# Four small moves in a hand-written instruction order: batch 7's attention beside the crossed products

## The chip, the cores and the metric

The kernel runs on one core of a Trainium2 chip. A core has five engines that run their own instruction lists in order and meet only at semaphores: TensorE (matrix products, shown as PE, its weight loads as PEld), VectorE (DVE), ScalarE (ACT), GpSimd (POOL) and SyncE (SP, which here only issues transfers). The metric is the device time of one execution in microseconds (us).

## The reference

Two layers follow one another. The first is a linear attention over 8 batches, 8 heads, 576 positions and 64 channels; the second mixes positions through a rank of 32 and then channels through two matrices, with a residual.

```python
r = relu(x);  phi(x) = concat([r * cos_w, r * sin_w])      # 64 -> 128 features
q_p, k_p = phi(q), phi(k)
kv  = einsum('bhsf,bhsd->bhfd', k_p, v)
num = einsum('bhsf,bhfd->bhsd', q_p, kv)
den = einsum('bhsf,bhf->bhs', q_p, k_p.sum(2)) + 1e-6
x   = (num / den), heads side by side                       # [8, 576, 512]

u   = x + ((x^T @ U) @ V)^T                                 # rank 32 over positions
out = u + relu(u @ w_ch1) @ w_ch2                           # 512 -> 2048 -> 512
```

## The kernel before

**Tiles.** A batch has 576 positions: four chunks of 128 (c = 0 to 3) and a tail of 64 (c = 4). The tails of two batches make one tile of 128, so there are four pairs of tails. The first matrix has 16 column blocks of 128 (j), each a `g1_main` unit: four products of 128x512 (L579) and a relu on ScalarE (L588). The second matrix is worked through in two halves per batch by `half_part`: seven products per half, where a plain product would need eight, each a group of eight matmuls of 128x256 (L891). Their operand sums (`hid_sum`, L833) are on VectorE. For batch 7, and for blocks 4 to 7 and 12 to 15 of batch 6, the first matrix is worked through with seven products (`g1_cross`, L676), with sums of uT and of the weights (L611, `uT_sum`, `w1_sum`).

**The crossed steps.** In `g1_cross` and `g1_join`, a block p has a bank "xy" (columns 0 to 255 are X, the rest is Y) and a bank Z. `opened` writes products 1 (X) and 2 (Y), then ScalarE casts X to `kept` ("P1") and VectorE adds it to Y ("C11"). `sixth` accumulates product 6 on X and casts it ("U2"); `fifth` writes Z and casts it ("P5"); `third` accumulates on X, and VectorE adds it to P5 ("C22"); `closed` accumulates on Z and X, followed by the add "C12" and a relu on VectorE, and a relu on ScalarE.

**Attention of a later batch.** `attention_plan` spreads the next batch's attention over the slots of the batches before it. For batch 7 (base slot 189) it holds two kv units, five x units (chunk order 4, 0, 1, 2, 3), the A unit (x^T U, L445), u (`u_mm`, L475, and `u_add`, L483), the tails' u (`u_tail`, L497 and L504) and transposes on SP's queue (`utr_dma`, L521 and L527). An x unit is eight matmuls (L422) into a tile of two banks tagged "X", then on VectorE rec, a reciprocal and the normalisation (L412, L413, L432). `u_mm` for columns 0 to 2, `u_mm` for column 3, and `u_tail` likewise, take this same X tile, so each waits for what reads it.

**The order.** It is written out by hand. `slots` is a list of TensorE steps; `todo[i]` holds what is issued right behind slot i. The instructions of a slot go to the engines in program order, so a slot number says both when a step's matmuls come and where its VectorE, ScalarE and SP work stands in those engines' queues. Batch 6's first stage begins at slot 188: two g1 units, then in turn a `half_part` of batch 5 (even slots) and a unit of batch 6 (odd slots). Slots 218 to 220 are `tail_late(2)`, the last `closed` of batch 6 and `tail_late(3)`: units of the first matrix for the tails of batches 4 and 5. From slot 221 on the groups of batch 7's crossed products alternate with `half_part` of batch 6. The number of slots up to here also sets where `uT_sum` of batch 7 and the operand sums of batch 6 are placed (`at`).

Of the kernel before, what the change touches and what calls it, by code (L numbers as in the profile page):

```python
# [17 lines left out]
def kernel(  # L18
# [13 lines left out]
    B = 8  # L32
# [13 lines left out]
    def tail(b):  # L46
        lo = TS * (b % 2)
        return slice(lo, lo + TS)
# [290 lines left out]
    def kv_unit(b, hg, tag, bufs, eng=None, n=E):  # L339
        if b not in kv_sb:  # L340
            kv_sb[b] = pool.tile([P, H, E], BF16, tag="kv", bufs=2, name="kv")
        acc = ps.tile([P, 4, n], FP32, tag=tag, bufs=bufs, name="kv_ps")
        vx = v_ext
        for i in range(4):
            h = hg * 4 + i
            for c in range(5):
                nc.tensor.matmul(  # L347
                    out=acc[:, i, :],
                    lhsT=k_of(b, c, h),
                    rhs=v_tl[:, h, 0:n] if c == 4 and b < 2  # L350
                    else vx[:, c if c < 4 else 4 + b % 2, h, 0:n],
                    start=(c == 0),
                    stop=(c == 4),
                )
        cast(eng or V_, kv_sb[b][:, hg * 4 : hg * 4 + 4, 0:n], acc)
# [83 lines left out]
    def A_of(b):  # L439
        return A_sb[b % 4]  # L440
# [16 lines left out]
    def four_banks(*spare):  # L457
        t = ps.tile([P, 2, 512], FP32, tag="X", bufs=1, name="va4_ps")
        more = [
            x if not isinstance(x, tuple)  # L460
            else ps.tile([P, 512], FP32, tag=x[0], bufs=x[1], name="va_ps")
            for x in spare
        ]
        return [t[:, 0, :], t[:, 1, :]] + more
# [3 lines left out]
    def u_mm(b, *spare, js=range(4)):  # L468
        if b not in u_bf:
            u_bf[b] = pool.tile([P, 4, 4, P], BF16, tag="u_bf", bufs=3, name="u_bf")  # L470
        va.setdefault(b, {}).update(zip(js, four_banks(*spare)))
        for c in range(4):
            for j in js:
                rows = slice(j * R, j * R + R)
                nc.tensor.matmul(  # L475
                    out=va[b][j][:, c * P : c * P + P], lhsT=V_bf[rows, c, :],
                    rhs=A_of(b)[rows, :], start=(c == 0), stop=(c == 3),
                    tile_position=(j * R, 0),
                )
# [8 lines left out]
    def u_tail(pr, *spare, js=range(4)):  # L488
        if pr not in u_tl:
            u_tl[pr] = pool.tile(  # L490
                [P, DM], BF16, tag="k_p" if pr == 3 else "u_tl", bufs=1, name="u_tl"
            )
        vt = dict(zip(js, four_banks(*spare)))
        for i in range(2):
            for j in js:
                rows = slice(j * R, j * R + R)
                nc.tensor.matmul(  # L497
                    out=vt[j][tail(i), 0:P], lhsT=V_tl[rows, :],
                    rhs=A_of(2 * pr + i)[rows, :], start=True, stop=True,
                    tile_position=(j * R, i * TS),  # L500
                )
        for j in js:
            ns = slice(j * P, j * P + P)
            nc.vector.tensor_tensor(  # L504
                out=u_tl[pr][:, ns], in0=x_tl[:, ns], in1=vt[j][:, 0:P], op=ALU.add
            )
# [475 lines left out]
    def spare(at):  # L982
        if at < 72:
            return ("o", 2) if 32 <= at < 52 else ("g", 3)
        return ("o", 2) if at < 88 else ("s", 1)
# [14 lines left out]
    def attention_plan(b):  # L1000

        plan = []
        if b < 4:
            w, f_at, q_eng, k_eng, qtr, lo = PLAN[b]
        else:
            w, q_at, k_at, qtr, lo = PLAN[b]

        def put(at, f, *a, tag=False):
            if tag:
                a = a + spare(w + at)  # L1010
            plan.append((w + at, lambda: f(b, *a)))

        for n, c in enumerate(QORD):
            if b > 3:
                put(q_at[0] + q_at[1] * n, q_prep, c, q_at[2:])
                put(k_at[0] + k_at[1] * n, k_prep, c, k_at[2:])
                put(k_at[0] + (3 * n) // 2, v_prep, 0, H, (c,), (G_,))
                continue
            if b == 3:
                q_eng, k_eng = V_ if n == 3 else A_, A_ if n < 3 else None  # L1020
                put((-12, -11, -10, -7, -3)[n], q_prep, c, (q_eng, q_eng))
                put(n - 9 if n < 3 else -5, k_prep, c, (A_, k_eng))
                if n > 2:
                    put(2 * n - 12, k_prep, c, (None, V_))
                put(-4 if n > 2 else -6, v_prep, 0, H, (c,), (A_ if n > 2 else G_,))
                continue
            put(f_at + ((n - 1) % 5 if b == 2 else n), q_prep, c, (q_eng, q_eng))
            put(f_at + 6 + n, k_prep, c, (k_eng, k_eng))
            put((-6, -2, -1, -5, -5)[n], v_prep, 0, H, (c,), (V_ if n > 2 else A_,))
        for n, (c0, c1) in enumerate(((4, 5), (0, 2), (2, 4))):  # L1030
            at = qtr[n] if b > 4 else 1 if b == 3 and n == 2 else qtr + 2 * n
            put(at, qtr_dma, c0, c1)
        plan.append((w + (b == 2), lambda: kv_unit(b, 0, *spare(w), A_ if b > 2 else V_)))
        plan.append((w + 2, lambda: kv_unit(b, 1, *spare(w + 2), A_ if b > 2 else V_)))
        for n, c in enumerate(ORD):
            if b > 3:
                put(4 + 2 * n, x_unit, c, "X", 1)
            elif n % 2:
                put(9 if (b, n) == (3, 3) else 4 + (3 * n) // 2, x_two, c, tag=True)
            else:  # L1040
                put(4 + (3 * n) // 2, x_unit, c, "X", 1)
        a_at = 15 - b if b < 4 else 14
        if b == B - 1:
            put(a_at, A_unit, "s", 1, A_)
        else:
            put(a_at, A_unit, tag=True)
        odd = b % 2 == 1


        def two(at):  # L1050
            return [T1, ("s", 1)] if at >= 88 else [spare(at)] * 2

        if b == B - 1:
            plan.append((w + a_at + 2, lambda: u_mm(b, ("s", 1), js=(0, 1, 2))))
            plan.append((w + a_at + 4, lambda: u_mm(b, js=(3,))))
        else:
            plan.append((w + a_at + 2, lambda: u_mm(b, *two(w + a_at + 2))))
        for j in range(4):
            put(a_at + 2 + j + (2 if b > 4 and j > 1 else 0), u_add, j)
        put(a_at + 3, utr_dma, 0, 2)  # L1060
        put(a_at + (7 if b > 4 else 5), utr_dma, 2, 4)
        if odd:
            if b == B - 1:
                plan.append((w + a_at + 9, lambda: u_tail(b // 2, ("s", 1), js=(0, 1, 2))))
                plan.append((w + a_at + 10, lambda: u_tail(b // 2, js=(3,))))
            else:
                plan.append((w + a_at + 9, lambda: u_tail(b // 2, *two(w + a_at + 9))))
            put(a_at + 10, utr_dma, 4, 5)
        for at, t in zip(lo, loads(b + 1) if lo else ()):
            plan.append((w + at, t))  # L1070
        return plan
# [264 lines left out]
    slots, todo = [], {}  # L1336

    def put(at, thunk):
        todo.setdefault(at, []).append(thunk)

    def sums(b, n, ats):
        for i, at in enumerate(ats):
            put(at, lambda i=i: hid_sum(b, n, i + 1))
# [31 lines left out]
    for b in range(3, B - 2):  # L1375
        at = len(slots)
# [15 lines left out]
    b6, b7 = B - 2, B - 1  # L1392
# [30 lines left out]
    def crossed(*steps):  # L1423
        def go():
            for f, b, p in steps:
                f(b, p)

        return go
# [9 lines left out]

    at = len(slots)
    sums(b6 - 1, 0, (at, at + 1, at + 3))  # L1440
    sums(b6 - 1, 1, (at + 13, at + 15, at + 19))
    for i, half, sl in (
        (1, 1, -8), (2, 1, -6), (3, 1, -4), (1, 0, -3), (4, 1, -2), (3, 0, -1), (2, 0, 11), (4, 0, 23),
    ):
# [15 lines left out]
    def tail_late(j):  # L1460
        if j == 2:
            t = ps.tile([P, 2, 512], FP32, tag="X", bufs=1, name="gt_ps")[:, 0, :]
        else:
            t = ps.tile([P, 512], FP32, tag="s", bufs=1, name="gt_ps")
        g1_tail(2, j, t.rearrange("p (j t) -> p j t", j=4))

    slots.append(lambda: tail_late(2))
    slots.append(crossed((closed, b6, 7)))
    slots.append(lambda: tail_late(3))

    at = len(slots)
    for i in range(4):
# [16 lines left out]

    for i, go in enumerate(groups):  # L1490
        slots.append(go)
        if i < 14:
            beside_g(b6, i)
        else:
            slots.append(lambda j=i - 14: tail_cross(j))
    at = len(slots)
# [16 lines left out]
    at = len(slots)  # L1513
# [19 lines left out]
    for b in range(2, B):  # L1533
        for at, t in attention_plan(b):
            put(at, t)
# [37 lines left out]
```

## Time and profile before

| what | value |
|---|---|
| median of 3 runs | 296.16 us (296.05 to 298.54) |
| the profiled execution's own time | 296.26 us |
| its span, first to last instruction | 294.5 us |
| mean granted TensorE clock | 0.997 |
| busy: PE, PEld | 284.8 us, 194.6 us |
| busy: DVE, ACT, POOL | 207.5 us, 169.3 us, 57.8 us |
| slots 192 to 203 in the trace | about 213.4 to 226.8 us |
| batch 7's first crossed step | 242.74 us |
| start of the last stage (`half_part` of batch 7 alone) | 271.85 us |
| last TensorE group starts, last VectorE add | 289.31 us, 290.39 us |

Rows of the trace name an engine, a source line, an operation and its tiles (`a_ps` is the A unit's accumulator, `va_ps` that of u and the tails' u, `c_ps` of the crossed products, `h_ps` of `half_part`, `S` an operand sum). Where many steps share a helper, they have that helper's line, and tiles and order tell them apart. The bracket at the end of a row is the time that the engine stood idle ahead of it, and what ended that. A busy TensorE may still wait inside: matmuls are pipelined, and the end of one overlaps the start of the next.

### The profile page before, as it was taken

The page shows a single profiled execution, that of the slowest core. Times are in us where ns is not written, and L with a number is a line of the kernel's source. Part 1 is how long each engine was busy: PE and PEld are TensorE (multiplying, and loading weights), DVE is VectorE, ACT ScalarE, POOL GpSimd, SP SyncE. Part 2 cuts the span into 40 slices and gives each one's busy share as a digit, 9 for nine tenths or more (in the row PEclk, how much of TensorE's full clock was granted, in tenths as well). Part 3 has the DMA queues.
Part 4 walks back from the last instruction along what each step waited for, and adds up shares of the span by engine and source line. Part 5 has one row for each costly group of instructions (what it writes and reads, how often), then busy time and mean ns, then how long its engine had stood idle before and what let it go on. Part 6 is the DMA issues. An engine that isn't in the chain of part 4 may idle for free.

```text
span 294.5 us, 7310 instructions
## 1 busy us (share of the span) xinstructions
PE 284.8 (97%) x2910; PEld 194.6 (66%) x2944; DVE 207.5 (70%) x503; ACT 169.3 (57%) x353; POOL 57.8 (20%) x92
## 2 busy tenths in 40 slices
PE   8999999999999999999999999999998999999994
PEld 3775554447545446766766666766776778889883
DVE  5977855596875698566457774779866877775773
ACT  3955742276782767488647764687643546557210
POOL 6520600000020005103200500042103213303330
PEclk9999999999999999999999999999999999999998
DMA  7999999899998989997899759874902744336023
GB/s 232 297 254 251 273 166 212 217 298 232 351 190 200 288 183 262 265 304 237 145 246 270 201 119 270 214 257 92 213 1 39 145 89 108 48 98 137 9 101 116
DMA packets 95174, 56.18 MB, mean 191 GB/s; under 512 B 58692, under 2 KB 91844, under 8 KB 95140
## 3 DMA queue, kind: packets, MB, share of 16 engines
q1 hardware_dynamic: 84420, 43.94, 59.7%
q0 software_dynamic: 10528, 11.57, 19.6%
q8 instruction: 23, 0.38, 0.5%
q10 hardware_dynamic: 192, 0.20, 0.2%
q14 instruction: 11, 0.09, 0.1%
HBM read 36.86 MB, written 9.44 MB: 157 GB/s over the span
## 4 chain that ended last, share of the span: by engine, by line
PE 94%; DVE 3%; issue 1%; ACT 0%; DVEq 0%
PE g_ps L579 29%; PE h_ps L891 26%; PE o_ps L759 10%; PE c_ps L676 6%; PE gt_ps L719 5%; PE kv_ps L347 3%; PE w_ps L234 3%; PE x_ps L422 3%; PE h_ps L759 1%; PE a_ps L445 1%; PE g_ps L596 1%; PE va_ps L475 1%; PE t_ps L365 1%; PE t_ps L377 1%; PE z_ps L1236 1%
## 5 line engine op out<-in xcount | busy, mean ns | idle before, releaser
L579 PE MATMUL g_ps<-uT,w_bf 128*128 128x512 bf16 x378 | 95.5, 380 | 1.1
L588 ACT ACTIVATE hid<-g_ps 128x512 bf16<-128x512 f32 x104 | 61.0, 598 | 57.1 <-PE g_ps L579 56.3
L579 PEld LDWEIGHTS <-w_bf 128*128 128x128 bf16 x402 | 37.8, 98 | 34.7 <-issue 0.2
L891 PEld LDWEIGHTS <-hid 128*128 128x128 bf16 x480 | 45.3, 98 | 9.0
L891 PE MATMUL h_ps<-w_bf,hid 128*128 128x256 bf16 x288 | 37.1, 273 | 0.0
L759 PE MATMUL o_ps<-w_bf,hid 128*128 128x512 bf16 x122 | 29.5, 380 | 0.4 <-issue 0.2
L131 POOL CAST v_ext<-vst 128x512 bf16<-128x512 f32 (+1 forms) x23 | 15.5, 700 | 58.2 <-issue 25.7
L891 PE MATMUL h_ps<-w_s,S 128*128 128x256 bf16 x208 | 26.5, 273 | 0.0
L891 PE MATMUL h_ps<-w_s,hid 128*128 128x256 bf16 x192 | 24.9, 273 | 0.0
L611 DVE TENSOR_TENSOR hid<-kept,c_ps 128x256 bf16<-128x256 f32 x36 | 14.2, 418 | 12.5 <-ACT kept L129 9.1
L847 DVE TENSOR_TENSOR o_sb<-o_sb,h_ps 128x256 f32<-128x256 f32 (+1 forms) x36 | 15.4, 431 | 10.7 <-PE h_ps L891 8.3
L891 PEld LDWEIGHTS <-S 128*128 128x128 bf16 x208 | 19.9, 98 | 4.0
L950 POOL DMA_DIRECT2D out_dram<-o_sb x16 | 10.1, 631 | 62.8 <-DVE o_sb L847 51.7
L483 DVE TENSOR_TENSOR u_bf<-x_bf,va_ps 128x512 bf16<-128x512 bf16 x27 | 17.6, 680 | 6.5 <-PE va_ps L475 2.8
L847 DVE TENSOR_TENSOR o_sb<-u_bf,h_ps 128x256 f32<-128x256 bf16 x28 | 11.7, 416 | 13.2 <-PE h_ps L891 13.2
L759 PEld LDWEIGHTS <-hid 128*128 128x128 bf16 x128 | 11.5, 98 | 12.2
L949 POOL DMA_DIRECT2D o_sb<-u_bf x8 | 10.4, 1295 | 36.6 <-DVE o_sb L847 35.5
L719 PE MATMUL gt_ps<-uT_tl,w_bf 128*128 128x128 bf16 x256 | 16.2, 219 | 0.0
L432 DVE TENSOR_TENSOR x_bf<-x_ps,rec 128x512 bf16<-128x512 f32 x22 | 15.2, 691 | 0.8
L719 PEld LDWEIGHTS <-w_bf 128*128 128x128 bf16 x256 | 15.1, 98 | 0.7
L129 ACT ACTIVATE kept<-c_ps 128x256 f32<-128x256 f32 x36 | 12.5, 380 | 4.9 <-PE c_ps L676 4.1
L306 ACT ACTIVATE k_p<-kst,cosw 128x512 bf16<-128x512 f32 x20 | 14.2, 713 | 0.1
(189 smaller groups left out, 457.6 us busy)
## 6 DMA issues: line engine op xcount, KB each, us to landing
qst<-in_q_dram SPq DMA_DIRECT2D x14, 512.0 KB, 5.4
kst<-in_k_dram SPq DMA_DIRECT2D x14, 512.0 KB, 6.5
vst<-in_v_dram SPq DMA_DIRECT2D x12, 512.0 KB, 6.7
out_dram<-o_sb POOLq DMA_DIRECT2D x19, 256.0 KB, 4.1
out_dram<-o_sb SPq DMA_DIRECT2D x16, 256.0 KB, 2.6
w_bf<-in_moe_w_ch_dram POOLq DMA_DIRECT2D x7, 512.0 KB, 12.4
o_sb<-u_bf POOLq DMA_DIRECT2D x8, 256.0 KB, 3.6
qst<-in_q_dram SPq DMA_DIRECT2D x2, 640.0 KB, 13.6
```

The costliest lines, as they stand in the source:

```text
L131: eng.tensor_copy(out=o, in_=i)
L306: nc.scalar.activation(out=o, in_=i, func=AF.Relu, bias=0.0, scale=w)
L432: nc.vector.tensor_tensor(out=x_of(b, c, rows).rearrange("p (g i d) -> p g i d", g=2, d=D), in0=view[:, :, :, 0:D], in1=rec[rows].unsqueez ...
L483: nc.vector.tensor_tensor(out=u_bf[b][:, j, :, :], in0=x_bf[b][:, :, ns], in1=va[b][j].rearrange("p (c n) -> p c n", c=4), op=ALU.add,)
L579: nc.tensor.matmul(out=g_ps.rearrange("p (c t) -> p c t", c=4), lhsT=w1_bf[:, d, j * P : j * P + P], rhs=uT[b][:, d, :, :], start=(d == 0) ...
L588: nc.scalar.activation(out=hid[b][:, j, :], in_=g_ps, func=AF.Relu, bias=0.0, scale=1.0)
L611: V_.tensor_tensor(out=o, in0=x, in1=y, op=op)
L676: nc.tensor.matmul(out=w[to].rearrange("p (c t) -> p c t", c=2), lhsT=lhs[:, d, cs], rhs=rhs[:, d], start=(first and d == 0), stop=(d == 1 ...
L719: nc.tensor.matmul(out=g_ps[:, jj, :], lhsT=w1_bf[:, d, j * P : j * P + P], rhs=uT_tl[pr][:, d, :], start=(d == 0), stop=(d == 3),)
L759: nc.tensor.matmul(out=o[:, cols], lhsT=lhs[:, j, c * P : c * P + P], rhs=w2_bf[:, j, cols], start=(j == 0), stop=(j == NJ - 1),)
L847: eng.tensor_tensor(out=o, in0=x, in1=y, op=ALU.add)
L891: nc.tensor.matmul(out=acc, lhsT=lhs[:, j, :], rhs=rhs[:, j, :], start=(j == 0 and at is not None), stop=(j == 7), skip_group_check=at is ...
```

## The change

Five parts of the order change; no arithmetic does.

- Batch 7's five x units go from slots 193, 195, 197, 199, 201 to 192, 194, 196, 198, 200.
- The first two operand sums of the second half of batch 5 go from slots 201 and 203 to 202 and 204.
- Column 3 of batch 7's `u_mm` goes from slot 207 to 208, behind the `half_part` of slot 208. Its `u_add` stays at slot 210.
- Column 3 of the last pair's `u_tail` goes from slot 213 to 214, and the transpose of that pair's tails with it.
- `tail_late(3)` goes from slot 220 to 221, behind the first group of batch 7 (`opened(7, 0)`), which goes from 221 to 220. Because `at` is taken ahead of it, batch 7's four uT sums go from slots 217 to 220 to 216 to 219, and the sums of batch 6 from 221, 222, 227 and 234, 236, 240 to 220, 221, 226 and 233, 235, 239. From slot 222 on the TensorE steps have their old numbers.

```diff
-                put(4 + 2 * n, x_unit, c, "X", 1)
+                put((3 if b == B - 1 else 4) + 2 * n, x_unit, c, "X", 1)
...
-            plan.append((w + a_at + 4, lambda: u_mm(b, js=(3,))))
+            plan.append((w + a_at + 5, lambda: u_mm(b, js=(3,))))
...
-                plan.append((w + a_at + 10, lambda: u_tail(b // 2, js=(3,))))
+                plan.append((w + a_at + 11, lambda: u_tail(b // 2, js=(3,))))
...
-            put(a_at + 10, utr_dma, 4, 5)
+            put(a_at + (11 if b == B - 1 else 10), utr_dma, 4, 5)
...
-    sums(b6 - 1, 1, (at + 13, at + 15, at + 19))
+    sums(b6 - 1, 1, (at + 14, at + 16, at + 19))
...
     slots.append(lambda: tail_late(2))
     slots.append(crossed((closed, b6, 7)))
-    slots.append(lambda: tail_late(3))
 
     at = len(slots)
...
     for i, go in enumerate(groups):
         slots.append(go)
+        if i == 0:
+            slots.append(lambda: tail_late(3))
         if i < 14:
             beside_g(b6, i)
```

## The prediction, made before the result was known

> **What bounds the kernel now.** I read the page's busy times and chain first, then TensorE's waits, then the order of time of TensorE, VectorE and ScalarE between 213 and 245 us, where all the edits lie.
>
> ```profile
> PE 284.8 (97%) x2910; PEld 194.6 (66%) x2944; DVE 207.5 (70%) x503; ACT 169.3 (57%) x353; POOL 57.8 (20%) x92
> PE 94%; DVE 3%; issue 1%; ACT 0%; DVEq 0%
> ```
>
> TensorE carries 94% of the chain that ended last, so the matmuls stay and only its stalls can go. Three of the six waits in its list lie here:
>
> ```profile
> PE a_ps L445 <- DVE x_bf L432: 0.9, 1, 0.9
> PE va_ps L497 <- DVE u_tl L504: 0.5, 1, 0.5
> PE va_ps L475 <- DVE u_bf L483: 0.5, 1, 0.5
> ```
>
> In TensorE's order of time the columns are start, duration and operation. Groups overlap, so I work with steps from one start to the next: 0.87 us for a g1 unit (x4, 128x512) or a product of half_part (x8, 128x256), 0.26 for an x unit, 0.22 for one crossed product (x2).
>
> ```profile
> 222.30 1.03 PE L579 MATMUL g_ps<-uT,w_bf 128*128 128x512 bf16 x4
> 223.17 0.60 PE L676 MATMUL c_ps<-uT,w_bf 128*128 128x256 bf16 x4
> 223.60 0.42 PE L422 MATMUL x_ps<-kv,q_pT 128*128 128x65 bf16 x8
> 223.86 1.04 PE L891 MATMUL h_ps<-w_s,hid 128*128 128x256 bf16 x8
> 225.02 0.38 PE L676 MATMUL c_ps<-uT_s,w_s 128*128 128x256 bf16 x2
> ...
> 226.66 0.24 PE L445 MATMUL a_ps<-x_bf,U_bf 128*32 128x128 bf16 x4 [0.93 <-DVE x_bf L432]
> ...
> 231.18 0.39 PE L475 MATMUL va_ps<-A_sb,V_bf 32*128 32x128 bf16 x4 [0.46 <-DVE u_bf L483]
> ...
> 237.49 0.24 PE L497 MATMUL va_ps<-A_sb,V_tl 32*64 32x128 bf16 x2 [0.50 <-DVE u_tl L504]
> ```
>
> There is a fourth stall that the list of waits does not name: 243.17 + 0.87 = 244.04, but the next group starts at 244.31. VectorE's order of time shows what each one waited for:
>
> ```profile
> 224.55 0.42 DVE L611 TENSOR_TENSOR hid<-kept,c_ps 128x256 bf16<-128x256 f32 x1 [1.46 <-ACT kept L129]
> 224.88 0.69 DVE L833 TENSOR_TENSOR S<-hid 128x1024 bf16<-128x1024 bf16 x1
> ...
> 225.92 0.69 DVE L432 TENSOR_TENSOR x_bf<-x_ps,rec 128x512 bf16<-128x512 f32 x1
> ...
> 230.44 0.68 DVE L483 TENSOR_TENSOR u_bf<-x_bf,va_ps 128x512 bf16<-128x512 bf16 x1
> ...
> 243.84 0.42 DVE L611 TENSOR_TENSOR hid<-kept,c_ps 128x256 bf16<-128x256 f32 x1 [0.33 <-ACT kept L129]
> ```
>
> The last x normalisation (225.92 to 226.61) stood behind the first join (224.55) and an operand sum (224.88), though its matmuls were over at 224.02. The group at 244.31 began 0.05 us after the join of 243.84 ended.
>
> **The change part by part.** No instruction is added or removed; the gain can only come from these stalls.
>
> *x units a slot sooner.* Each x unit now runs ahead of its slot's g1 unit. The first starts at 213.39 + 0.87 = 214.26; its kv cast on ScalarE ended at 213.98. VectorE follows: output add at 214.52, operand sum 214.86, then rec, reciprocal and x_tl from 215.19 at the old steps (0.21, 0.23, 0.69), ending at 216.32. x(0) needs that bank; the old start came 0.15 after the release (217.04, 217.19), so it starts at 216.47 where TensorE is ready at 216.26. That is a wait of 0.21, against 0.07 before. The later x units have 0.3 or more to spare. Slot 201's crossed products then end at 224.01 in place of 223.86: -0.15.
>
> Now a wait grows. The sixth product (225.02) starts 0.05 after the join of 224.55 ended. The chain to it starts with the g1 unit's relu and runs on through the P1 cast and that join. The x unit used to fill 0.26 of this time and is gone from there. New chain: g1 at 222.71, relu 1.07 later at 223.78 to 224.38, P1 cast 0.16 later (as before, 223.97 to 224.13) until 224.92, join 224.96 to 225.38, sixth product at 225.43. TensorE is free at 224.88, so it waits 0.55, against 0.29 before.
>
> Behind it, batch 7's A unit no longer waits: x(3) is normalised by about 224.1, ahead of the join in VectorE's order. Sixth product 0.22, change of operation 0.09, A unit 0.39 (as at 193.93 to 194.32): half_part starts at 226.13 in place of 226.84. **Gain 0.71.** The 0.16 ahead of the cast may belong to the x unit that moved; without it the gain is 0.87. The first join reads columns 256 to 511 of the bank and the sixth product writes columns 0 to 255. If only columns counted, the P1 cast (ended 224.51, +0.05) would release it, and the gain would be 1.17. I take 0.71, since 225.02 follows the join by the 0.05 us of the other releases.
>
> The Trainium skill, PSUM — Partial Sum Buffer, section Terms, speaks against this part in the same way: TensorE writing and VectorE reading one bank and quadrant at once is an error, so the scheduler must hold the product behind the join whatever the columns. By that rule the part gives 0.71, without it 1.17; the row at 225.02 agrees with the rule.
>
> *The two sums.* They moved from slots 201 and 203 to 202 and 204. Only ScalarE casts lie between on the evacuating engines, so VectorE's order is unchanged, and with the x work gone it reaches them sooner, with 1.56 us of idle behind them: nothing. A reordering cost could not exceed that idle.
>
> *u's last part a slot later.* Before, TensorE is ready at 230.56 and would start at 230.66 (0.10 for a change of operation, as 228.59 to 228.69), but it waits until 231.18 for the add of 230.44, which frees the X banks. After, half_part fills this time: 230.56 + 0.87 + 0.10 + 0.32 = 231.85 for the next crossed product, before 232.39. **Gain 0.54**; the cover left is 231.53 against 231.12, 0.41 us. The join after it has less cover: VectorE is free at 232.92, the join would start at 232.96. The last add stays at slot 210, so the transpose issued behind it on SP's queue keeps its place.
>
> *The tails' u a slot later.* Before: ready 236.82, start 237.49, half_part 237.66, next crossed product 238.53. After: 236.82 + 0.87 + 0.10 + 0.17 = 237.96, 0.57 sooner. Then the closing product (0.22 later, 238.18) meets the C22 join that ended at 238.30; with 0.05 that costs 0.17. **Gain 0.40** (0.57 if that join comes sooner). On SP only the tails' transpose moves, and its readers start at 266.71.
>
> *Batch 7's first step ahead of the last late tail unit.* The tail unit (0.90) now fills the time to the join. P1 cast, join (0.42) and 0.05 end well within the 0.90 + 0.87 us to the next product: **gain 0.27**. Cover 0.36 us, by VectorE: this step and the uT sums are a slot sooner, so a sum goes ahead of the C12 join. Batch 6's sums are one slot sooner too; only the third passes a join, into VectorE's idle 0.57 us at 247.57. ScalarE's evacuation of the tail unit (0.60) now follows the cast, and its bank is next wanted two groups later.
>
> Sum 0.71 + 0.54 + 0.40 + 0.27 = 1.92. From 244.31 on the order is the same and TensorE leads, so all of it should reach the end. The profiled execution took 296.26 (span 294.5 and 1.76 around it): 296.26 - 1.92 = 294.34, **294.3 us**. The median shown is 296.16, 0.10 less.
>
> **The rivals.** *VectorE takes over as the bound.* It is busy 6.00 of the 6.81 us from 232.39 to 239.20, nearly all one stretch behind the join of 233.50. If the join there comes no sooner, the second and third gains are lost: 0.98 is left, 295.3. Against: VectorE stood idle 0.52 ahead of that join, and 1.56 ahead of 228.77.
>
> *Slower: the transpose of batch 7's second half.* The first step needs both halves of uT, and now runs 2.56 us sooner (242.74 to 240.18), while the transpose, issued at 235.5, is 1.25 sooner. VectorE's second sum would start at 239.65, 5.4 us after the issue at 234.25. The trace shows landings of 2.7 and 4.2 us for uT, and 8.5 in the median for the larger q_pT. At 8.5 it lands at 242.75; two sums, the C12 join and its relu (0.42, 0.45, 0.45 and 0.50 in steps) bring half_part to about 244.6 in place of 241.51: 3.1 lost, 297.4. It starts to cost beyond 5.4 us and eats the whole gain at about 7.3. Unlikely, since nothing else of this size moves on SP.
>
> *No change that counts:* the saved waits return one group later because accumulator banks, not the named joins, are short: 296.2. The first stall alone speaks against it, as its bank chain was followed above.
>
> *More:* the gains of 1.17 and 0.57 come true: 293.7.
>
> **How the numbers follow.** Forecast 0.60; VectorE 0.20; no change 0.09; more 0.06; slower 0.05. From 293.6, just under the best sum, to 296.1, short of no change, holds some 0.85. A difference of 1% (2.96 us) is about what a measurement tells from none. Faster by that needs 293.2, beyond the best sum by 0.5: 0.05. Slower comes from the transpose, in which 297.4 is itself only 0.4% up, so it keeps 0.03.
>
> **What would show it.** Right: no wait of a_ps, and none of va_ps on u_bf or u_tl; the sixth product at about 225.4, the next half_part near 226.1; the product of 244.31 near 242.4; equal spacing from there. A longer gap ahead of the sixth product, or joins that begin with VectorE busy, would show the first rival; uT sums or opened products that wait for a DMA near 240 the second. Wrong altogether would be a start of the last stage (271.85) that does not move by about 1.9.

## The result, and the profile after

| | before | after |
|---|---|---|
| median | 296.62 us (10 runs) | 294.63 us (10 runs) |
| ratio, 95% interval | | 0.9933 (0.991 to 0.9957) |
| profiled execution, its span | 296.26, 294.5 us | 294.76, 293.0 us |
| start of slot 192's half_part | 213.39 us | 213.67 us |
| start of the last stage | 271.85 us | 270.33 us |
| between these two ("the stretch") | 58.46 us | 56.66 us |

The kernel is 1.99 us faster by the medians. All edits lie in the stretch, and there it gained 1.80; what comes ahead of the stretch was 0.28 longer in this execution, although no instruction there changed. The rows of the kernel before from which the stretch and its steps are read:

```profile
213.39 1.04 PE L891 MATMUL h_ps<-w_bf,hid 128*128 128x256 bf16 x8
...
226.84 1.05 PE L891 MATMUL h_ps<-w_bf,hid 128*128 128x256 bf16 x8
...
232.39 0.60 PE L676 MATMUL c_ps<-uT,w_bf 128*128 128x256 bf16 x4
...
239.20 1.04 PE L891 MATMUL h_ps<-w_s,hid 128*128 128x256 bf16 x8
...
243.17 1.04 PE L891 MATMUL h_ps<-w_bf,hid 128*128 128x256 bf16 x8
244.31 0.60 PE L676 MATMUL c_ps<-uT_s,w_s 128*128 128x256 bf16 x4
...
271.85 1.91 PE L891 MATMUL h_ps<-w_bf,hid 128*128 128x256 bf16 x16
```

The page of the changed kernel, busy times:

```profile
PE 284.9 (97%) x2910; PEld 194.5 (66%) x2944; DVE 206.6 (71%) x503; ACT 169.2 (58%) x353; POOL 56.6 (19%) x92
```

TensorE did the same work in a shorter span. Its list of waits in the changed kernel (engine, operation, releaser: total, times, longest):

```profile
PE c_ps L676 <- DVE hid L611: 0.4, 1, 0.4
PE x_ps L422 <- DVE x_tl L432: 0.2, 1, 0.2
```

The waits of a_ps on x_bf and of va_ps on u_bf and u_tl are gone, and two others have come. The order of time of TensorE in the changed kernel (start, duration, operation, idle time ahead); 0.28 has to be taken off a start to set it against one of before:

```profile
213.67 1.04 PE L891 MATMUL h_ps<-w_bf,hid 128*128 128x256 bf16 x8
...
215.67 1.04 PE L891 MATMUL h_ps<-w_s,S 128*128 128x256 bf16 x8
216.87 0.42 PE L422 MATMUL x_ps<-kv,q_pT 128*128 128x65 bf16 x8 [0.17 <-DVE x_tl L432]
...
223.97 0.60 PE L676 MATMUL c_ps<-uT,w_bf 128*128 128x256 bf16 x4
224.41 1.04 PE L891 MATMUL h_ps<-w_s,hid 128*128 128x256 bf16 x8
225.82 0.38 PE L676 MATMUL c_ps<-uT_s,w_s 128*128 128x256 bf16 x2 [0.38 <-DVE hid L611]
...
226.53 1.05 PE L891 MATMUL h_ps<-w_bf,hid 128*128 128x256 bf16 x8
...
231.22 0.39 PE L475 MATMUL va_ps<-A_sb,V_bf 32*128 32x128 bf16 x4
231.54 0.61 PE L676 MATMUL c_ps<-uT,w_bf 128*128 128x256 bf16 x4
...
237.13 0.39 PE L676 MATMUL c_ps<-uT,w_s 128*128 128x256 bf16 x2
237.52 0.38 PE L676 MATMUL c_ps<-uT_s,w_bf 128*128 128x256 bf16 x2
...
237.95 1.04 PE L891 MATMUL h_ps<-w_s,hid 128*128 128x256 bf16 x8
...
241.92 1.04 PE L891 MATMUL h_ps<-w_bf,hid 128*128 128x256 bf16 x8
242.79 0.60 PE L676 MATMUL c_ps<-uT_s,w_s 128*128 128x256 bf16 x4
...
270.33 1.91 PE L891 MATMUL h_ps<-w_bf,hid 128*128 128x256 bf16 x16
```

Reading it with the steps of the prediction: x(0), the second x unit, at 216.87 is 0.33 later than its half_part lets it (215.67 + 0.87); the sixth product at 225.82 is 0.54 later than 224.41 + 0.87; u's last part now starts straight behind its half_part; the closing product comes 0.39 behind the one ahead, in place of 0.22; and 242.79 follows 241.92 by the plain 0.87, so the fourth stall is gone.

VectorE's order of time in the changed kernel:

```profile
215.14 0.42 DVE L611 TENSOR_TENSOR uT_s<-uT,uT_s 128x512 bf16<-128x512 bf16 x1
215.59 0.17 DVE L412 TENSOR_SCALAR rec<-x_ps 64x8 f32<-64x8 f32 x1
...
216.03 0.69 DVE L432 TENSOR_TENSOR x_tl<-x_ps,rec 64x512 bf16<-64x512 f32 x1
...
223.85 0.69 DVE L432 TENSOR_TENSOR x_bf<-x_ps,rec 128x512 bf16<-128x512 f32 x1
225.35 0.42 DVE L611 TENSOR_TENSOR hid<-kept,c_ps 128x256 bf16<-128x256 f32 x1 [0.80 <-ACT kept L129]
```

The last x normalisation (223.85) now stands ahead of the join (225.35), so the A unit finds it done. The join ends at 225.77 and the sixth product starts at 225.82.

### The profile page after: what moved, and what is told of

It reads as the page before. It is cut to its first block, busy times and chain, and to the rows that moved or that the text cites. A ratio compares the mean times of both kernels' runs of the same rounds, so it can differ in the third digit from the quotient of the medians.

```text
span 293.0 us, 7309 instructions
## 1 busy us (share of the span) xinstructions
PE 284.9 (97%) x2910; PEld 194.5 (66%) x2944; DVE 206.6 (71%) x503; ACT 169.2 (58%) x353; POOL 56.6 (19%) x92
## 4 chain that ended last, share of the span: by engine, by line
PE 91%; ACT 3%; DMA 2%; DVE 2%; issue 1%; ACTq 0%; DVEq 0%
PE g_ps L579 29%; PE h_ps L891 26%; PE o_ps L759 10%; PE c_ps L676 7%; PE gt_ps L719 5%; PE kv_ps L347 3%; PE x_ps L422 3%; DMA qst<-in_q_dram 2%; PE a_ps L445 1%; PE h_ps L759 1%; PE g_ps L596 1%; PE va_ps L475 1%; PE t_ps L365 1%; ACT q_p L306 1%; ACT k_p L306 1%
## 5 line engine op out<-in xcount | busy, mean ns | idle before, releaser
L891 PEld LDWEIGHTS <-hid 128*128 128x128 bf16 x480 | 45.6, 98 | 9.5
L891 PE MATMUL h_ps<-w_bf,hid 128*128 128x256 bf16 x288 | 37.1, 273 | 0.0
L891 PE MATMUL h_ps<-w_s,S 128*128 128x256 bf16 x208 | 26.5, 272 | 0.0
L891 PE MATMUL h_ps<-w_s,hid 128*128 128x256 bf16 x192 | 24.9, 273 | 0.0
L891 PEld LDWEIGHTS <-S 128*128 128x128 bf16 x208 | 20.1, 98 | 4.4
```

What stands on the lines that cost most here:

```text
L891: nc.tensor.matmul(out=acc, lhsT=lhs[:, j, :], rhs=rhs[:, j, :], start=(j == 0 and at is not None), stop=(j == 7), skip_group_check=at is ...
```

## The experiments

The runs are compared by the stretch, from slot 192's half_part to the first product of the last stage. It came out as 56.66 in both profiles of the changed kernel, while whole times of one kernel spread over 2 us.

### Each part alone

The four parts that could gain were put into the kernel before one at a time.

```diff
 x alone
-                put(4 + 2 * n, x_unit, c, "X", 1)
+                put((3 if b == B - 1 else 4) + 2 * n, x_unit, c, "X", 1)
 u alone
-            plan.append((w + a_at + 4, lambda: u_mm(b, js=(3,))))
+            plan.append((w + a_at + 5, lambda: u_mm(b, js=(3,))))
 tails' u alone
-                plan.append((w + a_at + 10, lambda: u_tail(b // 2, js=(3,))))
+                plan.append((w + a_at + 11, lambda: u_tail(b // 2, js=(3,))))
...
-            put(a_at + 10, utr_dma, 4, 5)
+            put(a_at + (11 if b == B - 1 else 10), utr_dma, 4, 5)
 first step alone
-    slots.append(lambda: tail_late(3))
...
+        if i == 0:
+            slots.append(lambda: tail_late(3))
```

> Only the x units of batch 7 a slot sooner; the rest as before. Measured by one stretch of the profile: from the start of slot 192's product of half_part to the first product of the last stage (58.46 us before, 56.66 after the whole change). Theory A (separate TensorE stalls that add up): the a_ps wait of 0.93 goes, the sixth product's wait grows from 0.29 to about 0.55, x(0) waits 0.2 to 0.3; the stretch is 0.59 shorter, 57.87. Rival (columns, not the bank, hold the sixth product): 1.0 or more shorter. Rival (VectorE is the bound behind it): the va_ps waits on u_bf and u_tl grow by what is saved, the stretch stays within 0.15 of 58.46.

> Only column 3 of batch 7's u a slot later. Same stretch (58.46 us before). Theory A: the va_ps wait on u_bf goes and nothing comes in its place, 0.54 shorter, 57.92. Rival (VectorE is the bound): the join that began at 233.50 comes no sooner, so the waits on u_tl or of the closing products grow; the gain is under 0.2.

> Only column 3 of the tails' u and its transpose a slot later. Same stretch (58.46 us before). Theory A: the va_ps wait on u_tl goes (0.57), the closing product of slot 215 waits about 0.17 for the C22 join in its place: 0.40 shorter, 58.06. Rival (the join comes soon enough): 0.57 shorter, 57.89. Rival (VectorE bound): under 0.15.

> Only batch 7's first step ahead of the last late tail unit, with the sums that move with it. Same stretch (58.46 us before). Theory A: the gap of 0.27 ahead of the next crossed product goes, 58.19. Rival (the transpose of batch 7's second half is needed too soon): uT sums or the opened products wait for a DMA, the stretch is no shorter or grows by up to 3.

| part | forecast | alone: stretch, gain | inside the whole change |
|---|---|---|---|
| x units | 0.71 | 57.85, 0.61 | 0.59 |
| u's last part | 0.54 | 57.92, 0.54 | 0.54 |
| tails' u | 0.40 | 58.03, 0.43 | 0.40 |
| first step | 0.27 | 58.19, 0.27 | 0.27 |
| sum | 1.92 | 1.85 | 1.80 |

The last column is read from the starts of four operations, counted from the start of the stretch: half_part behind the A unit (13.45 before, 12.86 after), the crossed product behind u's last part (19.00, 17.87), the half_part of slot 216 (25.81, 24.28) and the product of 244.31 (30.92, 29.12). Each step of the difference is the gain of one part: the difference grows 0.59, 1.13, 1.53, 1.80 and then stays 1.80 to the last stage. The whole times of these single executions (295.78, 298.60, 295.57 and 295.72 us, beside 300.01 of the kernel before) spread by more than the parts are worth. In the stretch the steps that an edit does not touch repeat: with the first step alone, every half_part up to slot 216 starts within 0.01 us of where it does in the kernel before.

TensorE's waits in the stretch, x alone:

```profile
PE va_ps L497 <- DVE u_tl L504: 0.5, 1, 0.5
...
PE va_ps L475 <- DVE u_bf L483: 0.5, 1, 0.5
PE c_ps L676 <- DVE hid L611: 0.4, 1, 0.4
PE x_ps L422 <- DVE x_tl L432: 0.2, 1, 0.2
```

The same view, u alone:

```profile
PE a_ps L445 <- DVE x_bf L432: 0.9, 1, 0.9
...
PE va_ps L497 <- DVE u_tl L504: 0.5, 1, 0.5
```

Each part removes its own wait and leaves the others as they were: VectorE does not hand a saved wait on to the next place. The two new waits of the changed kernel both come with the x units. The columns-only reading (a gain of 1.0 or more) falls with the 0.61.

The two operand sums were not run. With them put back to slots 201 and 203, every engine's list of instructions is the same as the changed kernel's but for the numbering of buffers. The measured parts add up without them.

### What holds the sixth product: a bank of its own for Y

```diff
             cross[b, p] = {"X": xy[:, 0:256], "Y": xy[:, 256:512], "of_z": of_z}
+            if (b, p) == (B - 2, 4):
+                y = psum.tile([P, 512], FP32, tag="g2", bufs=1, name="y_ps")
+                cross[b, p]["Y"] = y[:, 256:512]
...
-            2: lambda: ("Y", W1[1], uT_quarter(b, 1, 0), False),
+            2: lambda: ("Y", W1[1], uT_quarter(b, 1, 0), (b, p) == (B - 2, 4)),
```

> The changed kernel, with block 4's Y in a bank of its own, so that the join C11 of that block reads another bank than the one its sixth product writes. Same stretch (56.66 us in the changed kernel). Theory A (the sixth product is held by the join's read of the bank, whatever the columns): it then waits for the cast alone, which ended 0.46 sooner than the join: the wait of 0.54 shrinks to about 0.08, 56.2. Rival (it waits for the join's result, or for the operand sums): 56.66.

In the one execution of this version the stretch is 56.27, 0.39 shorter. TensorE and the join on VectorE with Y in its own bank (three lines were added above these, so L894 is L891 and L679 is L676):

```profile
225.44 1.04 PE L894 MATMUL h_ps<-w_s,hid 128*128 128x256 bf16 x8
226.31 0.38 PE L679 MATMUL c_ps<-uT_s,w_s 128*128 128x256 bf16 x2
...
226.16 0.42 DVE L611 TENSOR_TENSOR hid<-kept,y_ps 128x256 bf16<-128x256 f32 x1 [0.58 <-ACT kept L129]
```

The sixth product follows half_part without a wait, and it starts at 226.31, while the join still runs (226.16 to 226.58). The first product of the pair waits for VectorE in the changed kernel and for ScalarE here. So the join's read of the other half of the tile was what held it, not the join's result. Whether a bank or a tile is what the order is kept by is not told apart: in the changed kernel X and Y share both. The wait shrank to nothing in place of 0.08 because the cast began 0.54 after the start of the relu ahead (225.20, 225.74) and not 0.76 (224.17, 224.93); why it did was not traced. The half_part behind the A unit comes 0.53 sooner in the stretch, the last stage only 0.39: the closing product of slot 215 now starts 0.52 behind its neighbour (237.64, 238.16), against 0.39 in the changed kernel, so 0.13 went to VectorE's join there.

### The opened products ahead of the g1 unit

In slot 201 the chain to the sixth product starts with a g1 unit whose relu goes ahead of the cast. This version turns the two round, on top of the change.

```diff
-    units.append(lambda: [g1_main(b6, 11), opened(b6, 4)])
+    units.append(lambda: [opened(b6, 4), g1_main(b6, 11)])
```

> The changed kernel, with slot 201's two parts the other way round: the opened products of block 4 ahead of the g1 unit of block 11. Same stretch (56.66 us in the changed kernel). Theory A (the sixth product waits for the chain cast, join, and the bank): the chain now starts 0.87 sooner on TensorE and no longer stands behind the relu, so the wait of 0.54 ahead of the sixth product goes whole: 56.1. Rival (the sixth product waits for something else, its operand sums for one): the wait stays, 56.66. Rival (VectorE bound behind it): the wait goes but comes back in slots 207 to 215, 56.5 or more.

The stretch is 56.11, 0.55 shorter; the ratio to the kernel before is 0.99 (0.9866 to 0.9935), the median 294.08 (4 runs) beside 296.65 (17 runs). TensorE in this version:

```profile
223.08 0.60 PE L676 MATMUL c_ps<-uT,w_bf 128*128 128x256 bf16 x4
223.51 1.03 PE L579 MATMUL g_ps<-uT,w_bf 128*128 128x512 bf16 x4
224.38 1.04 PE L891 MATMUL h_ps<-w_s,hid 128*128 128x256 bf16 x8
225.25 0.38 PE L676 MATMUL c_ps<-uT_s,w_s 128*128 128x256 bf16 x2
```

Every start follows the one ahead by its plain step. The g1 unit now lies between the opened products and the sixth, and the whole 0.54 that the x units' move had left is gone. The operand sums, which are where they were, are ruled out as the cause.

### How much room VectorE has: one sum twice, and one sum moved

The weight sum of slot 211 (0.69 us on VectorE) stands in the dense stretch ahead of the closing product. It was made twice in the changed kernel, and moved to slot 216 in the swapped version.

```diff
 twice
         put(at + sl, lambda i=i, half=half: w1_sum(i, half))
+        if sl == 23:
+            put(at + sl, lambda i=i, half=half: w1_sum(i, half))
 moved
-        (1, 1, -8), (2, 1, -6), (3, 1, -4), (1, 0, -3), (4, 1, -2), (3, 0, -1), (2, 0, 11), (4, 0, 23),
+        (1, 1, -8), (2, 1, -6), (3, 1, -4), (1, 0, -3), (4, 1, -2), (3, 0, -1), (2, 0, 11), (4, 0, 28),
```

> The changed kernel with the weight sum of slot 211 made twice on VectorE: 0.60 us more of its work in the dense stretch, which leaves the result as it is. Same stretch (56.66 us in the changed kernel). If VectorE has no slack left there (it was idle 0.05 us from 228.5 to 238.9): TensorE waits about 0.6 more in slots 213 to 215, 57.2 to 57.3. If VectorE still has cover there: 56.66.

> As the swapped version, and the weight sum of 0.69 us on VectorE at slot 211 goes to slot 216, where VectorE stands idle 0.73 us. Theory A: the closing product of slot 215 no longer waits 0.17 for the C22 join; the stretch is 0.17 shorter than in the swapped version, 55.95, and the kernel about 0.7 us faster than the changed one, near 294.0 where that has 294.6. Rival (VectorE is not what that product waits for): as the swapped version, 56.1.

Twice, in one execution: 57.38, 0.72 longer. The pair takes 1.41 us in place of 0.69, and TensorE pays the 0.72 in full, in two places (0.42 more ahead of the first row than in the changed kernel, and 0.68 in place of 0.39 between the other two):

```profile
238.13 0.24 PE L497 MATMUL va_ps<-A_sb,V_tl 32*64 32x128 bf16 x2 [0.35 <-DVE u_tl L504]
238.30 0.39 PE L676 MATMUL c_ps<-uT,w_s 128*128 128x256 bf16 x2
238.98 0.38 PE L676 MATMUL c_ps<-uT_s,w_bf 128*128 128x256 bf16 x2 [0.29 <-DVE hid L611]
```

Moved: 55.97, 0.14 shorter than the swapped version. There the closing product came 0.38 behind its neighbour (236.57, 236.95); here it is 0.23:

```profile
237.60 0.39 PE L676 MATMUL c_ps<-uT,w_s 128*128 128x256 bf16 x2
237.83 0.38 PE L676 MATMUL c_ps<-uT_s,w_bf 128*128 128x256 bf16 x2
```

So after the change VectorE does bound this place, by 0.14 to 0.17, and the work added to it there was paid in full. In the changed kernel it is busy 10.30 of the 10.40 us from 228.50 to 238.90. The median of this version is 294.08 (6 runs), with a ratio of 0.99 (0.987 to 0.9931) to the kernel before: in whole time it cannot be told from the swapped one.

### The changed kernel again

> The changed kernel again, on the same chip as the versions beside it. 56.66 us in the stretch, and 1.8 to 2.0 us under the kernel before.

On the chip of these versions the stretch is 56.66 again; the median is 294.94 (12 runs) against 296.65 (17 runs), a ratio of 0.9932 (0.9909 to 0.9955). The forecast of 1.8 to 2.0 under the kernel before came out as 1.71.

### The wait of x(0)

On top of the last version, batch 6's fourth uT sum goes a slot later.

```diff
-        put(at + 1 + i, lambda i=i: uT_sum(b6, i + 1))
+        put(at + 1 + i + (i == 3), lambda i=i: uT_sum(b6, i + 1))
```

> The version with the swapped parts and the later weight sum, and batch 6's fourth uT sum a slot later, behind the first x unit's normalisation on VectorE. Same stretch (55.97 us in the version without this). Theory A (x(0) waits because VectorE's normalisation of the first x unit stands behind that sum, 0.45 from its start to the next): x_tl ends 0.45 sooner, before TensorE is ready for x(0); the wait of 0.33 goes, 55.64, near 293.8 us in all. Rival (x(0) waits for something else): 55.97.

The stretch is 55.78, only 0.19 shorter. TensorE in this version:

```profile
217.27 1.04 PE L891 MATMUL h_ps<-w_s,S 128*128 128x256 bf16 x8
218.14 0.42 PE L422 MATMUL x_ps<-kv,q_pT 128*128 128x65 bf16 x8
...
219.26 1.04 PE L891 MATMUL h_ps<-w_s,S 128*128 128x256 bf16 x8
220.26 0.43 PE L422 MATMUL x_ps<-kv,q_pT 128*128 128x65 bf16 x8
```

The wait of x(0) is gone, as theory A says (218.14 is 217.27 + 0.87). But the sum now stands ahead of x(0)'s normalisation (219.52 to 220.21), and x(1) waits 0.13 for it: 220.26 in place of 220.13. The rest of the miss, 0.01, is within reading. The whole time was 294.42 (6 runs) beside 296.52 (11 runs), a ratio of 0.9922 (0.9902 to 0.9943): by its stretch this is the shortest of all, by its whole time it cannot be told from the two before it.

## Why the prediction was right, step by step

**The bound.** TensorE's stalls were all there was to gain, and they were separate: the parts' gains add up to 1.85 alone and 1.80 together, against 1.92. The forecast of 294.3 stands beside a profiled 294.76 and a median of 294.63. Of the 0.46 to the profiled execution, 0.12 is the sum's own error and 0.28 lies ahead of the stretch. That the medians differ by 1.99, nearly the forecast 1.92, is partly chance: the executions of the kernel before spread over 2.7 us, and in the later pair the medians differ by 1.71. The stretch is the better witness, with 1.80.

**x units: 0.71 forecast, 0.59 measured.** This is the one term that was mis-sized. The wait of x(0) was put at 0.21 and measured 0.33. VectorE's step from the operand sum of 215.14 to rec was taken as 0.33, the step of before to another sum; it was 0.45 (215.14 to 215.59). The trace of before had shown it: there this same rec began 0.03 after the operation ahead of it had ended (215.19 + 0.69, then 215.91), so a step of 0.33, in which the two overlap, could not be taken for it. Batch 4's rec for its tail does overlap by 0.08 in that trace (127.08 + 0.42, then 127.42); it works on partitions 0 to 63 and batch 7's on 64 to 127, but that this makes the difference was not tested. The rest of this part held: the sixth product's wait was put at 0.55 and was 0.54, the cast came 0.16 behind the relu (224.77 to 224.93), so the 0.16 did not belong to the moved x unit, and the A unit found x(3) done. What made the wait, named in the prediction as the join's read of the shared bank, was shown by giving Y a bank of its own, up to the question of bank or tile. The Trainium skill, PSUM — Partial Sum Buffer, section Terms, calls a TensorE write and a VectorE read of one bank and quadrant at the same time an error. The trace agrees with keeping the two apart: alone the part gained 0.61, not 1.0 or more, and only with Y in another bank did the product start during the join.

**u's last part: 0.54, measured 0.54.** The cover held as well. The join behind it began straight behind VectorE's third sum (232.67, with that sum's start at 231.99), at the limit that the prediction named, and cost nothing.

**The tails' u: 0.40, measured 0.40.** The new wait of the closing product was put at 0.17 and is 0.17 (237.13 to 237.52, less the plain 0.22). That the C22 join makes it is borne out by the moved sum, which took 0.14 of it away.

**The first step: 0.27, measured 0.27.**

**The two sums: nothing.** They change no engine's order, so there was nothing to measure.

**The rivals.** VectorE as the bound was the nearest: it does set the closing product's time, but by the 0.17 that the prediction's sum had already counted. The transpose did not come late: it was issued at 234.6, uT's landings in this part took 2.7 to 3.9, and the first sum of uT starts at 238.57; its readers wait for ScalarE and for one another, and no product or sum waits for a DMA. The saved waits did not return one group later, as the steady 1.80 from 242.79 to the last stage shows.

## What to carry to other kernels

Where one engine carries the chain, look for its stalls in the order of time and not in the list of waits alone, which left out one of the four here; for each, name the work that will fill it and the next thing that this work makes late, and the gains can be added up to 0.1 us. Moving filler out of one gap opens another: at their old place the x units' 0.26 had been hiding part of the chain to the sixth product, and turning two units round was worth almost as much as that whole part of the change. For sub-microsecond edits compare a fixed stretch between two landmarks, since the opening moves the whole time by more.

## What had not been expected of the hardware

The stretch came out the same to 0.01 us in two profiles of the changed kernel on different occasions, while the time ahead of it did not. The first g1 unit began between 22.92 and 25.77 us in the twelve profiled executions, with the same instructions ahead of it. From there to the stretch ten of them agreed within 0.3 us (190.20 to 190.51); the two others (the later uT sum, and Y's own bank) took 191.74 and 191.77. In those two TensorE has waits there that the ten lack: with the later uT sum 0.5 us for a transpose of q to land and 0.4 for an add on VectorE, with Y's own bank 1.0 and 0.3 for VectorE's preparation of q. What made these late stays open. The kernel with u alone has the latest opening, 2.8 us later than that of the profile of before, and with it 298.6 us of whole time although its stretch is 0.54 shorter than before. In that execution ScalarE waited 0.8 us for k and 0.8 us for v to land, and TensorE 0.8 us for each of the operations behind, which the kernel before did not; so 1.6 of these 2.8 us came from loads that landed late. This is why whole times needed many runs here, and the stretch one.
